# LayerNorm on GpSimd as scale and add in a fused attention and GLU block, with a re-planned instruction order

## The chip, the cores and the metric

The kernel runs on one core of one Trainium2 chip. The time is the device time of one execution in microseconds; the time before is the median of three runs, 234.61 us (234.28 to 237.68). One further execution was taken by the profiler; its span is 233.8 us and its own time 235.49 us.

## The reference, cut to what matters

One transformer block on x of 2048 rows and 512 columns in bf16: an adaptive LayerNorm (scale and shift come from a vector c through `w_mod`), linear attention with 32 heads of 16 whose feature map is a pair of softmaxes, a second adaptive LayerNorm, and a gated linear unit with 1376 hidden columns.

```python
h = layernorm(x) * (1 + ca) + sa              # (x - m) / sqrt(v + eps), then scale, shift
q, k, v = split(h @ wqkv)                     # 32 heads of 16
phi(t) = [softmax(t @ w_phi), softmax(-t @ w_phi)]
kv, z = phi(k)^T v, sum of phi(k) over rows
x = x + ga * ((phi(q) kv) / (phi(q) z + 1e-6)) @ wo
h = layernorm(x) * (1 + cb) + sb
x = x + gb * (sigmoid(h @ w_gate) * (h @ w_up)) @ w_down
```

## The kernel before

The rows are cut into 16 tiles of 128 rows (t = 0 to 15). Everything stays in SBUF. The work falls into two parts.

The K/V loop goes over the tiles in nine groups (LG: tiles 0 and 1 alone, then pairs). For each tile: VectorE takes mean and variance (`st1`, L782 and L783, into `mv1`); a group's `rs1` = 1/sqrt(v + eps) is made by Ln and Exp on ScalarE (L789, L790) or by add and power on GpSimd (L792, L793); `nmr` = -mean x rs1 is made by VectorE (L799); the normalised tile `xn` is made on ScalarE (L808, as rs1 x + nmr), VectorE (L810) or GpSimd (L812), the last two as (x - mean) rs1. `xn` is transposed, by TensorE into PSUM (`tp_h`, L826) or by a DMA on SyncE's queue (L818) for groups 2, 6 and 7, and scaled and shifted into `h1T` in four pieces (L833 on ScalarE, L835 on VectorE or, for DMA groups, GpSimd). TensorE then makes K (L853, with w_phi folded into the weights, `fold_ps`, L758) and V (L857); ScalarE takes exp of +K and -K (`e`, L869); VectorE sums each head's 16 columns (`ks`, L872); the reciprocal is made on VectorE (L885) or as Ln and Exp on ScalarE (L882, L883); GpSimd multiplies (`phi`, L875), in NPART pieces for a tile; TensorE accumulates `kvacc` (L343) with `vaug`, a copy of V (L893). The buffers of `e` and `phi` come from a class of six (r2k), so few tiles are in flight. Matmuls on a zeroed weight tile (`warm`, L710) keep TensorE running at the start. modc (L722) is scale and shift of both LayerNorms; `bd` (L693) is the block diagonal of w_phi.

The second part goes over the tiles again: q and its exponentials (`q_ps` L927, `eT` L932), numerator and denominators (`num` L463, `sm` L438, `u` L469), the sum of both halves `o` on GpSimd (L487), its transposition by DMA (L490), the output projection (`a_ps` L496), the second LayerNorm, and the GLU in six chunks (`g_ps` and `u_ps` L581, `tg` L585, product L590, `y_ps` L604). GpSimd also scales wo by ga (L911) and w_down by gb (L916). At the end of the program stands a branch for inputs of a large range, which isn't taken.

Order and placement: every piece of work is a task with the engines it may run on and an estimated time for each (`alts`), a due time and a release time. `Graph.order` runs a list scheduler over them when the program is built: at each moment it takes the ready task of the earliest due time whose engine and buffers are free. The tables at the top (T0, KP, LGD, KD, UD, MISC, WARM and others) are due and release times; XN1, HM1 and RK say which engines each tile's `xn`, `h1T` pieces and reciprocals may use; XN1_T, and numbers in the calls of `G.add`, are the estimated times. On the chip each engine then runs its own list in order and waits by semaphores; the estimates matter there only through the order.

Of the kernel before, what the change touches and what calls it, by code (L numbers as in the profile page):

```python
# [56 lines left out]
KD = [47.89, 15.44, 5.38, 21.3, -5.65, -2.7, -0.87]
LGD = [4.09, -2.99, 1.74, 8.75, 21.66, 5.51, 6.02, -0.76, -1.68]
GSL = [4.41, 1.07, 0.25, 0.64, 1.79, 10.29]
UD = [-1.67, 1.09, -8.4, -21.5, 10.53, -7.46, 32.4, -7.3, -2.67]  # L60
MISC = [25.74, 36.7, 47.58, 53.98, -8.92, 22.77, 51.62]
# [163 lines left out]
def kernel(  # L225
# [550 lines left out]
    for g, ts in enumerate(LG):  # L776
# [18 lines left out]
        nmr_used = any(e == "ACT" for t in ts for e in XN1[t])  # L795
        if nmr_used:
            def f_nm(e, ts=ts):
                for t in ts:
                    dve.tensor_scalar(nmr[:, 0, t:t + 1], mv1[:, t, 0:1], rs1[:, t:t + 1], -1.0, op0=ALU.mult, op1=ALU.mult)  # L799
            G.add(f"nmr1_{g}", {"DVE": 0.07 * n}, f_nm,  # L800
                  r=[("rs1", g)], w=[("nmr1", g)], due=gd)
        for t in ts:
            xn = Buf("xn", [P, D], BF16, "xn")
            xns.append(xn)

            def f_xn(e, t=t, xn=xn):
                if e == "ACT":
                    act.activation(xn[:], x_sb[:, t, :], ACT.Identity, scale=rs1[:, t:t + 1], bias=nmr[:, 0, t:t + 1])  # L808
                elif e == "DVE":
                    dve.tensor_scalar(xn[:], x_sb[:, t, :], mv1[:, t, 0:1], rs1[:, t:t + 1], op0=ALU.subtract, op1=ALU.mult)  # L810
                else:
                    pool.tensor_scalar(xn[:], x_sb[:, t, :], mv1[:, t, 0:1], rs1[:, t:t + 1], op0=ALU.subtract, op1=ALU.mult)  # L812
# [228 lines left out]
```

## Time and profile before

| what | value |
|---|---|
| median of three runs | 234.61 us (234.28 to 237.68) |
| the profiled execution: time, span | 235.49 us, 233.8 us |
| TensorE busy | 208.6 us, 89% of the span |
| VectorE busy | 163.9 us, 70% |
| ScalarE busy | 108.6 us, 46% |
| GpSimd busy | 107.9 us, 46% |
| DMA moved | 19.02 MB, mean 81 GB/s |

The page cuts the span into 40 slices and gives each engine's busy share in a slice in tenths. Busy shares over the whole span mix the two parts, so stages are read one by one. In rows of instructions the columns are line, engine, operation, output and inputs with their shapes, count, then busy time in us, mean ns of one, and the idle time of the engine just before them with what ended it. Rows of the timeline begin with start and duration in us. SPq is SyncE's DMA queue, PEld TensorE's weight loads.

### The profile page before, as it was taken

The numbers are of one execution on the slowest core, as the hardware profiler recorded it, in microseconds if no ns is written. First come the engines' busy times: TensorE is split into PE (matmuls) and PEld (weight loads), VectorE is DVE, ScalarE is ACT, GpSimd is POOL, SyncE is SP. The second block draws the span as 40 slices with busy tenths as digits, with TensorE's granted clock in tenths as the row PEclk, the third lists the DMA queues.
The fourth block names the chain that finished last, engine by engine and source line by source line (L and its number), as shares of the span: only waits on it lengthen the run. The fifth ranks groups of instructions, "written<-read, shape, count | busy, mean of one in ns | idle before, by whom it ended". The sixth has DMA issues, their size and how long they took to land.

```text
span 233.8 us, 4338 instructions
## 1 busy us (share of the span) xinstructions
PE 208.6 (89%) x1559; PEld 115.8 (50%) x1583; DVE 163.9 (70%) x380; ACT 108.6 (46%) x247; POOL 107.9 (46%) x115
## 2 busy tenths in 40 slices
PE   7694793897899997999999998999999999999990
PEld 2452441633454664786776453444465444444460
DVE  3199885954873799997887678858879886334330
ACT  4298882787695988453272321442232150343100
POOL 4759999999999829785110044200004510000000
PEclk9999999599999999999999999999999999999998
DMA  6974691059600002006222023031002224000011
...
DMA packets 31455, 19.02 MB, mean 81 GB/s; under 512 B 21729, under 2 KB 29378, under 8 KB 31426
## 3 DMA queue, kind: packets, MB, share of 16 engines
...
q8 instruction: 14, 0.23, 0.4%
...
q10 hardware_dynamic: 530, 0.02, 0.1%
...
## 4 chain that ended last, share of the span: by engine, by line
PE 51%; POOL 16%; issue 10%; DVE 10%; ACT 9%; DMA 2%; POOLq 0%; DVEq 0%; ACTq 0%; SPq 0%
PE y_ps L604 14%; PE g_ps L581 13%; PE u_ps L581 13%; POOL phi L875 7%; POOL xn L812 6%; PE a_ps L496 4%; ACT e L869 3%; PE warm L710 3%; DVE u L469 2%; DMA oT<-o 2%; ACT eT L932 2%; DVE st L505 1%; DVE x L501 1%; PE num L463 1%; PE k_ps L853 1%
## 5 line engine op out<-in xcount | busy, mean ns | idle before, releaser
L585 ACT ACTIVATE tg<-g_ps 128x512 bf16<-128x512 f32 (+5 forms) x66 | 29.4, 453 | 71.2 <-PE g_ps L581 59.9
L590 DVE SCALAR_TENSOR_TENSOR wmod_sb<-tg,u_ps 128x512 bf16<-128x512 bf16 (+5 forms) x66 | 31.8, 503 | 18.5 <-PE u_ps L581 16.9
L604 PE MATMUL y_ps<-wd_sb,wmod_sb 128*128 128x512 bf16 (+2 forms) x180 | 43.7, 366 | 0.3
L487 POOL TENSOR_TENSOR o<-u 128x512 bf16<-128x512 f32 x14 | 17.5, 1270 | 50.2 <-DVE u L469 50.2
L581 PEld LDWEIGHTS <-wg_sb 128*128 128x128 bf16 (+1 forms) x264 | 23.8, 100 | 18.4
L875 POOL TENSOR_TENSOR phi<-e,ks 128x1024 bf16<-128x1024 bf16 (+2 forms) x21 | 31.4, 1512 | 0.5
L581 PEld LDWEIGHTS <-wu_sb 128*128 128x128 bf16 (+1 forms) x264 | 23.5, 100 | 15.7
L581 PE MATMUL g_ps<-wT_sb,wg_sb 128*128 128x512 bf16 (+3 forms) x130 | 26.7, 325 | 0.2
L581 PE MATMUL u_ps<-wT_sb,wu_sb 128*128 128x512 bf16 (+3 forms) x130 | 26.6, 325 | 0.1
L872 DVE TENSOR_REDUCE ks<-e 128x64 f32<-128x1024 bf16 (+2 forms) x21 | 19.6, 952 | 9.8 <-POOL phi L875 5.2
L812 POOL TENSOR_SCALAR xn<-x_sb,mv,rs 128x512 bf16<-128x512 bf16 x12 | 24.9, 2076 | 3.1 <-ACT rs L790 2.7
L604 PEld LDWEIGHTS <-wmod_sb 128*128 128x128 bf16 (+1 forms) x187 | 17.8, 98 | 16.4
L869 ACT ACTIVATE e<-k_ps 128x512 bf16<-128x512 f32 (+2 forms) x42 | 17.7, 507 | 10.0 <-POOL phi L875 6.7
L581 PE MATMUL g_ps<-wqk_sb,wg_sb 128*128 128x128 bf16 (+5 forms) x132 | 22.1, 290 | 0.1
L581 PE MATMUL u_ps<-wqk_sb,wu_sb 128*128 128x128 bf16 (+5 forms) x131 | 21.9, 290 | 0.1
L469 DVE TENSOR_TENSOR u<-num,cc 128x512 f32<-128x512 f32 (+1 forms) x32 | 20.2, 682 | 0.8 <-PE num L463 0.6
L613 DVE TENSOR_TENSOR ot<-y_ps,x 128x512 bf16<-128x512 f32 (+1 forms) x17 | 11.2, 657 | 11.1 <-PE y_ps L604 11.1
L853 PE MATMUL k_ps<-wqk_f,h1T 128*128 128x512 bf16 x59 | 16.3, 391 | 0.8 <-DVE h1T L835 0.5
L932 ACT ACTIVATE eT<-q_ps 128x512 bf16<-128x512 f32 x32 | 16.5, 615 | 0.8 <-PE q_ps L927 0.8
L496 PE MATMUL a_ps<-wo_sb,oT 128*128 128x512 bf16 x62 | 16.0, 380 | 0.9 <-DMA oT<-o 0.6
L857 PE MATMUL v_ps<-wv_sb,h1T 128*128 128x512 bf16 x63 | 16.3, 384 | 0.1
L343 PE MATMUL kvacc<-vaug,phi 128*128 128x68 bf16 x128 | 7.8, 208 | 8.3 <-POOL phi L875 8.2
(128 smaller groups left out, 286.4 us busy)
## 6 DMA issues: line engine op xcount, KB each, us to landing
...
x_sb<-in_A_x_dram SPq DMA_DIRECT2D x3, 512.0 KB, 9.2
...
wqk_sb<-in_A_wqkv_dram SPq DMA_DIRECT2D x2, 512.0 KB, 7.2
wmod_sb<-in_w_mod_dram SPq DMA_DIRECT2D x2, 512.0 KB, 6.5
```

Source lines behind the costliest of these rows:

```text
L469: dve.tensor_tensor(u[:], ps[:].rearrange("p (h d) -> p h d", d=DH), cc[:, q, s, :].unsqueeze(2).to_broadcast([P, H, DH]), op=ALU.mult)
L496: pe.matmul(ap_[:], lhsT=oT[:, j, :], rhs=wo_sb[:, j, :], start=(j == 0), stop=(j == KT - 1))
L581: pe.matmul(ps[:fsz, 0:n], lhsT=w[:, j, ft * P:ft * P + fsz], rhs=h[:, j, 0:n], start=(j == 0), stop=(j == KT - 1))
L585: G.add(f"tg{k}.{ft}", {"ACT": 0.13 + n * 0.00083}, lambda e, tg=tg, g_ps=g_ps, fsz=fsz, n=n: act.activation(tg[:fsz, 0:n], g_ps[:fsz, 0:n ...
L590: dve.scalar_tensor_tensor(hm_all[:fsz, hm[k].slot, ft, 0:n], tg[:fsz, 0:n], 1.0, u_ps[:fsz, 0:n], op0=ALU.add, op1=ALU.mult)
L604: pe.matmul(y[:, 0:c1 - c0], lhsT=hm_all[:fsz, hm[k].slot, ft, tl * P:(tl + 1) * P], rhs=wd_sb[:fsz, ft, c0:c1], start=(ft == 0), stop=(ft ...
L812: pool.tensor_scalar(xn[:], x_sb[:, t, :], mv1[:, t, 0:1], rs1[:, t:t + 1], op0=ALU.subtract, op1=ALU.mult)
L853: pe.matmul(kp[:], lhsT=h1T[:, j, t * P:(t + 1) * P], rhs=wqk_f[:, j, D:2 * D], start=(j == 0), stop=(j == KT - 1))
L869: act.activation(ee[:, ha:hb, s, :], kp[:, ha * DH:hb * DH].rearrange("p (h j) -> p h j", j=DH), ACT.Exp, scale=1.0 - 2.0 * s)
L872: dve.tensor_reduce(ks[:, ha:hb].rearrange("p h s -> p (h s)"), ee[:, ha:hb].rearrange("p h s j -> p (h s) j"), axis=AX.X, op=ALU.add)
L875: pool.tensor_tensor(ph[:, ha * 32:hb * 32].rearrange("p (h j) -> p h j", j=DH), ee[:, ha:hb].rearrange("p h s j -> p (h s) j"), ks[:, ha: ...
L932: act.activation(eT[cq][:, s * 4 + blk, :], qp[:], ACT.Exp, scale=1.0 - 2.0 * s)
```

## The change

On GpSimd the first LayerNorm is now rs1 x + nmr, one instruction with multiply and add, as ScalarE already does it. So nmr is needed by every tile that may run on GpSimd, and such a task waits for it. Some estimated times are new (xn on each engine, nmr, the two GpSimd tasks `perm` and `wo`, the exponentials of q), and the tables of due times, releases and allowed engines have new values throughout. The changed file is two lines shorter, so its lines stand two earlier.

```diff
@@ -27,43 +27,41 @@
-NPART = [1, 1, 1, 1, 1, 1, 1, 1, 1, 1, 1, 1, 2, 1, 2, 4]
-T0, KP, GL = 10.3, 3.07, -8.17
-WARM = [1.2, 2.75, 5.27, 2.7, 1.2, 4.52, 5.28, 2.92, 1.75, 3.49, 8.85, 6.48, 10.34, 8.21, 7.83, 6.77]
+NPART = [1, 1, 1, 1, 1, 1, 1, 1, 1, 1, 1, 4, 1, 2, 2, 2]
+T0, KP, GL = 12.02, 3.1, -9.09
+WARM = [1.51, 4.09, 5.7, 3.33, 1.89, 2.68, 5.52, 2.14, 1.2, 5.18, 8.38, 9.39, 9.77, 13.05, 8.64, 8.5]
...
 XN1 = [
-    ['POOL', 'ACT'], ['POOL'], ['POOL', 'ACT'], ['DVE', 'POOL', 'ACT'], ['DVE', 'POOL', 'ACT'], ['DVE', 'POOL'], ['POOL', 'DVE'], ['DVE', 'ACT'],
-    ['POOL', 'DVE', 'ACT'], ['POOL'], ['ACT', 'DVE'], ['POOL'], ['POOL', 'ACT', 'DVE'], ['DVE', 'ACT', 'POOL'], ['DVE', 'POOL'],
-    ['ACT', 'POOL', 'DVE'],
+    ['DVE'], ['ACT', 'POOL', 'DVE'], ['ACT', 'DVE', 'POOL'], ['POOL'], ['POOL', 'DVE', 'ACT'], ['POOL', 'ACT', 'DVE'], ['DVE', 'POOL'],
+    ['POOL', 'ACT', 'DVE'], ['ACT', 'DVE', 'POOL'], ['POOL'], ['POOL'], ['POOL'], ['ACT', 'DVE', 'POOL'], ['POOL', 'ACT', 'DVE'],
+    ['POOL', 'DVE', 'ACT'], ['ACT'],
 ]
-XN1_T = {"ACT": 0.75, "POOL": 0.8, "DVE": 0.33}
+XN1_T = {"ACT": 0.73, "POOL": 0.69, "DVE": 0.3}
...
@@ -792,12 +790,12 @@
                 pool.tensor_scalar(ve1[:, sl], mv1[:, sl, 1], 1e-5, None, op0=ALU.add)
                 pool.tensor_tensor(rs1[:, sl], ve1[:, sl], mhalf[:, sl], op=ALU.pow)
         G.add(f"rs1_{g}", RS1[g], f_rs, r=[("mv1", t) for t in ts], w=[("rs1", g)], due=gd)
-        nmr_used = any(e == "ACT" for t in ts for e in XN1[t])
+        nmr_used = any(e != "DVE" for t in ts for e in XN1[t])
         if nmr_used:
             def f_nm(e, ts=ts):
                 for t in ts:
                     dve.tensor_scalar(nmr[:, 0, t:t + 1], mv1[:, t, 0:1], rs1[:, t:t + 1], -1.0, op0=ALU.mult, op1=ALU.mult)
-            G.add(f"nmr1_{g}", {"DVE": 0.07 * n}, f_nm,
+            G.add(f"nmr1_{g}", {"DVE": 0.02 + 0.1 * n}, f_nm,
                   r=[("rs1", g)], w=[("nmr1", g)], due=gd)
         for t in ts:
             xn = Buf("xn", [P, D], BF16, "xn")
@@ -809,9 +807,9 @@
                 elif e == "DVE":
                     dve.tensor_scalar(xn[:], x_sb[:, t, :], mv1[:, t, 0:1], rs1[:, t:t + 1], op0=ALU.subtract, op1=ALU.mult)
                 else:
-                    pool.tensor_scalar(xn[:], x_sb[:, t, :], mv1[:, t, 0:1], rs1[:, t:t + 1], op0=ALU.subtract, op1=ALU.mult)
+                    pool.tensor_scalar(xn[:], x_sb[:, t, :], rs1[:, t:t + 1], nmr[:, 0, t:t + 1], op0=ALU.mult, op1=ALU.add)
             alts = {e: XN1_T[e] for e in XN1[t]}
-            G.add(f"xn1_{t}", alts, f_xn, r=[("rs1", g)] + ([("nmr1", g)] if "ACT" in alts else []), w=[("xn1", t)],
+            G.add(f"xn1_{t}", alts, f_xn, r=[("rs1", g)] + ([("nmr1", g)] if set(alts) != {"DVE"} else []), w=[("xn1", t)],
                   bufs=[xn], due=gd, port=("POOL", "DVE"))
```

The rest of the diff holds new values of LGD, KD, UD, HM1, RK and the like, and three estimates: `perm` 0.7 to 1.3, `wo` 1.28 to 1.1, the exponentials of q 1.2 to 1.0.

What the scheduler makes of it is read from the instruction lists. Of the 16 xn GpSimd had 12 and ScalarE 4; now GpSimd has 9, ScalarE 5 and VectorE 2 (tiles 0 and 1). Both lists hold 15 nmr. GpSimd makes rs1 for four groups (before: three) and two h1T pieces (before: four). phi has 12 whole tiles, six halves and four quarters; before 13, four and four.

GpSimd's list at the start of the K/V loop, from the block diagonal bd on. Before:

```order
L693 TENSOR_TENSOR bd<-wp_sb,bmask 128x512
L812 TENSOR_SCALAR xn<-x_sb,mv_78,rs_80 128x512 x3
L792 TENSOR_SCALAR ve_79<-mv_78 128x2
L793 TENSOR_TENSOR rs_80<-ve_79,mhalf 128x2
L812 TENSOR_SCALAR xn<-x_sb,mv_78,rs_80 128x512
L875 TENSOR_TENSOR phi<-e,ks 128x1024
L835 TENSOR_SCALAR h1T<-h1T,modc 128x256
L875 TENSOR_TENSOR phi<-e,ks 128x1024
L812 TENSOR_SCALAR xn<-x_sb,mv_78,rs_80 128x512
L792 TENSOR_SCALAR ve_79<-mv_78 128x2
L793 TENSOR_TENSOR rs_80<-ve_79,mhalf 128x2
L812 TENSOR_SCALAR xn<-x_sb,mv_78,rs_80 128x512
```

Now:

```order
L691 TENSOR_TENSOR bd<-wp_sb,bmask 128x512
L810 TENSOR_SCALAR xn<-x_sb,rs_80,nmr 128x512 x2
L790 TENSOR_SCALAR ve_79<-mv_78 128x2
L791 TENSOR_TENSOR rs_80<-ve_79,mhalf 128x2
L790 TENSOR_SCALAR ve_79<-mv_78 128x2
L791 TENSOR_TENSOR rs_80<-ve_79,mhalf 128x2
L810 TENSOR_SCALAR xn<-x_sb,rs_80,nmr 128x512
L873 TENSOR_TENSOR phi<-e,ks 128x1024 x2
L810 TENSOR_SCALAR xn<-x_sb,rs_80,nmr 128x512 x5
L790 TENSOR_SCALAR ve_79<-mv_78 128x2
L791 TENSOR_TENSOR rs_80<-ve_79,mhalf 128x2
L873 TENSOR_TENSOR phi<-e,ks 128x1024 x4
```

Two xn, not three, stand first (those of tiles 0 and 1 have gone to VectorE), and a third waits behind two rs; behind the first two phi five xn stand in a row, and then four phi, where xn and phi took turns before.

VectorE's list at the same place, from the statistics of an early tile to the second sum for phi (ks). Before:

```order
L782 BN_STATS st_77<-x_sb 128x6
L783 BN_AGGR mv_78<-st_77 128x2
L799 TENSOR_SCALAR nmr<-mv_78,rs_80 128x1 x2
L782 BN_STATS st_77<-x_sb 128x6
L783 BN_AGGR mv_78<-st_77 128x2
L872 TENSOR_REDUCE ks<-e 128x64
L893 CAST vaug_104<-v_ps 128x32x16
L799 TENSOR_SCALAR nmr<-mv_78,rs_80 128x1 x2
L782 BN_STATS st_77<-x_sb 128x6
L783 BN_AGGR mv_78<-st_77 128x2
L872 TENSOR_REDUCE ks<-e 128x64
```

Now:

```order
L797 TENSOR_SCALAR nmr<-mv_78,rs_80 128x1 x2
L780 BN_STATS st_77<-x_sb 128x6
L781 BN_AGGR mv_78<-st_77 128x2
L780 BN_STATS st_77<-x_sb 128x6
L781 BN_AGGR mv_78<-st_77 128x2
L780 BN_STATS st_77<-x_sb 128x6
L781 BN_AGGR mv_78<-st_77 128x2
L870 TENSOR_REDUCE ks<-e 128x64
L797 TENSOR_SCALAR nmr<-mv_78,rs_80 128x1 x2
L870 TENSOR_REDUCE ks<-e 128x64
L797 TENSOR_SCALAR nmr<-mv_78,rs_80 128x1 x2
L883 RECIPROCAL ks<-ks 128x64
```

The nmr of the two pairs whose rs1 GpSimd makes now stand behind one ks each. Ahead of this piece VectorE makes the xn of tiles 0 and 1, the second behind its two copies of wT_sb.

TensorE's list at the same place goes over tile pairs: V0, V1, K0, K1, then (after warm matmuls and transposes) kvacc of tile 0, V2, V3, kvacc of tile 1, the transposes of tiles 6 and 7, K2, K3. Before it was K0, V0, K1, V1, and later kvacc of tile 0, K2, kvacc of tile 1, V2.

GpSimd's list behind the loop, from the scalings of wo on, now:

```order
L909 TENSOR_TENSOR wo_sb<-wo_sb,ga_sb 128x512 x4
L914 TENSOR_TENSOR wd_sb<-wd_sb,wmod_sb 128x512 x7
L485 TENSOR_TENSOR o<-u 128x512 x2
L514 TENSOR_SCALAR ve_83<-mv_82 128x1
L515 TENSOR_TENSOR rs_84<-ve_83,mhalf 128x1
L914 TENSOR_TENSOR wd_sb<-wd_sb,wmod_sb 128x512 x4
```

Seven scalings of wd_sb (L914) stand ahead of the first two o, where there were two; behind them rs of tile 1 for the second LayerNorm and the other four scalings.

More of the change, by code (lines that the diff above doesn't have):

```diff
@@ L52 @@
 ]
 RK = [
-    ['ACT'], ['DVE', 'ACT'], ['ACT'], ['DVE'], ['ACT'], ['DVE', 'ACT'], ['ACT'], ['DVE'], ['ACT'], ['DVE'], ['DVE'], ['DVE', 'ACT'], ['DVE'],
-    ['ACT'], ['ACT', 'DVE'], ['DVE'],
-]
[L57 to L61, printed above, removed]
+    ['ACT'], ['ACT', 'DVE'], ['DVE'], ['ACT'], ['ACT', 'DVE'], ['DVE', 'ACT'], ['ACT'], ['DVE'], ['ACT', 'DVE'], ['ACT', 'DVE'], ['ACT'],
@@ L62 @@
+    ['DVE', 'ACT'], ['ACT', 'DVE'], ['ACT', 'DVE'], ['DVE', 'ACT'], ['ACT', 'DVE'],
+]
+KD = [48.44, 11.65, 6.7, 25.12, -3.51, -11.2, -0.78]
+LGD = [2.92, -6.82, 9.16, -1.34, 23.14, 16.31, 0.7, 11.25, -7.18]
+GSL = [2.48, 1.14, 0.29, 0.81, 0.08, 3.45]
+UD = [-1.67, 5.7, 7.31, -25.78, 8.16, -6.86, 23.5, -7.3, 15.4]
+MISC = [25.41, 35.64, 49.36, 52.17, -11.34, 27.03, 44.33]
 TD = [0, 0, 1, 0, 0, 0, 1, 1, 0]
@@ L65 @@
 ENG = {}
-WDREL, WDDUE, WDSTEP = 71.41, 142.51, 0.01
+WDREL, WDDUE, WDSTEP = 65.72, 186.99, -0.81
 class Buf:
@@ L356, in f @@
                     pool.tensor_copy(bd[:, 2 * s + h, h * 64:(h + 1) * 64].rearrange("p (h j) -> p h j", j=DH), iv[:, :, s, :])
-        G.add("perm", {"POOL": 0.7}, f, w=["bd"], due=due, rel=rel)
+        G.add("perm", {"POOL": 1.3}, f, w=["bd"], due=due, rel=rel)
     def kvbd_tasks(G, acc):
@@ L910 @@
     for j in range(KT):
-        G.add(f"wo{j}", {"POOL": 1.28}, lambda e, j=j: engine(e).tensor_tensor(wo_sb[:, j, :], wo_sb[:, j, :], ga_sb[:], op=ALU.mult),
+        G.add(f"wo{j}", {"POOL": 1.1}, lambda e, j=j: engine(e).tensor_tensor(wo_sb[:, j, :], wo_sb[:, j, :], ga_sb[:], op=ALU.mult),
               r=["gac", "wo_raw"], w=[("wo", j)], bufs=[ga_sb], due=GB + MISC[5], rel=50.0)
@@ L934 @@
             G.add(f"Q{cq}{blk}", {"PE": 0.87}, f_q, r=[("h1", g, j) for g in range(len(LG)) if LG[g][0] // 4 == cq for j in range(KT)] + [("wqk", j, 0) for j in range(KT)], w=[("q", cq, blk)], bufs=[qp], due=due, rel=QREL[cq])
-            G.add(f"qe{cq}{blk}", {"ACT": 1.2}, f_qe, r=[("q", cq, blk)], w=[("eT", cq, blk)], bufs=[qp, eT[cq]], due=due)
+            G.add(f"qe{cq}{blk}", {"ACT": 1.0}, f_qe, r=[("q", cq, blk)], w=[("eT", cq, blk)], bufs=[qp, eT[cq]], due=due)
     downstream(G, eT, GB, True)
```

18 lines of the change are left out of this document (8 added, 10 removed).

## The prediction

> **What bounds the kernel now.** I read the slices and the chain of the page first, then busy time by stage, then the waits of the first 90 us.
>
> ```profile
> POOL 4759999999999829785110044200004510000000
> PE 51%; POOL 16%; issue 10%; DVE 10%; ACT 9%; DMA 2%; POOLq 0%; DVEq 0%; ACTq 0%; SPq 0%
> ```
> ```profile
> core 0: us, PE busy (x) PEld busy (x) DVE busy (x) ACT busy (x) POOL busy (x), PEclk, DMA share, GB/s
> 15.40:73.10 57.70, 45.15 (x354) 23.59 (x358) 42.18 (x92) 42.33 (x104) 56.67 (x41) 0.94 0.48 145
> 73.60:97.30 23.70, 21.67 (x243) 14.26 (x245) 21.04 (x51) 18.91 (x42) 17.95 (x21) 1.00 0.06 12
> 97.30:228.60 131.30, 129.55 (x868) 71.60 (x879) 93.58 (x218) 39.63 (x81) 24.80 (x29) 1.00 0.19 42
> 40.00:50.00 10.00, 7.77 (x91) 5.07 (x93) 7.68 (x16) 7.93 (x22) 9.92 (x7) 0.66 0.14 29
> ```
> ```profile
> PE kvacc L343 <- POOL phi L875: 8.2, 8, 4.0
> ACT e L869 <- POOL phi L875: 6.7, 2, 4.2
> DVE ks L872 <- POOL phi L875: 5.2, 4, 3.2
> ```
>
> The kernel has two parts. From 73.6 on, TensorE sets the end: 21.67 of 23.70 us busy, then 129.55 of 131.30. In the K/V loop, 15.40 to 73.10, GpSimd does: 56.67 of 57.70 us, while the other three are busy for 42 to 45 us and wait for phi, the GpSimd product. TensorE's work is the same either way, so what shortens the loop should move everything behind it forward.
>
> **What GpSimd does in the loop.** Groups by form: count, busy us, mean ns, idle before.
>
> ```profile
> L875 POOL TENSOR_TENSOR phi<-e,ks 128x1024 bf16<-128x1024 bf16 x13 | 25.0, 1927 | 0.3
> L875 POOL TENSOR_TENSOR phi<-e,ks 128x512 bf16<-128x512 bf16 x4 | 4.1, 1055 | 0.2
> L875 POOL TENSOR_TENSOR phi<-e,ks 128x256 bf16<-128x256 bf16 x4 | 2.4, 618 | 0.0
> L812 POOL TENSOR_SCALAR xn<-x_sb,mv,rs 128x512 bf16<-128x512 bf16 x12 | 24.9, 2076 | 3.1 <-ACT rs L790 2.7
> L835 POOL TENSOR_SCALAR h1T<-h1T,modc 128x256 bf16<-128x256 bf16 x4 | 2.2, 555 | 0.0
> L793 POOL TENSOR_TENSOR rs<-ve,mhalf 128x2 f32<-128x2 f32 x3 | 2.2, 718 | 0.3
> L516 POOL TENSOR_SCALAR ve<-mv 128x2 f32<-128x2 f32 x7 | 1.5, 220 | 23.8 <-DVE mv L506 23.8
> ```
>
> Ten of the twelve xn fall behind 15.40: 10 x 2.076 = 20.8; phi 25.0 + 4.1 + 2.4 = 31.5; h1T 2.2; three times rs with its add of eps, 3 x 0.94 = 2.8. Sum 57.3, the whole window. So a microsecond off GpSimd here is a microsecond off the loop, until another engine is as long.
>
> **The price of the new xn.** No row shows scale-and-add at 128x512. The nearest is h1T on the same engine: the same instruction with two per-partition fp32 operands, bf16 in and out, multiply then add, at 256 columns 555 ns; subtract then multiply costs 2076 at 512. Twice the columns cannot make 3.7 times the time, so the pair of operations must carry most of it. Below: the line through the 2-column add (220 ns) and h1T gives 555 + 256 x 335/254 = 893 ns. Above: twice h1T, 1110, and if the shape rather than the operations is slow, 2076. I take 950, nearest to the line. As a side note, the Trainium skill (GPSIMD Engine Reference, section 3.1, Elementwise) gives one-input loops a best case of 769 ns for 512 elements, whatever the operation; by that the nine xn would cost 6.9 us, not 8.6. The 2076 row shows that operation pairs do differ here, which the page does not say.
>
> **What moves.** On GpSimd 12 xn become 9 (3 x 2.076 and 9 x 1.126 saved), h1T pieces 4 become 2, rs groups 3 become 4; phi has 12 whole, 6 half and 4 quarter tiles, 31.9 us. From 57.3 + 2 x 2.076 = 61.5 us the queue shrinks to 8.6 + 31.9 + 1.1 + 3.8 = 45.4.
>
> The offsets cost nothing new: 15 of them stand in the trace and 15 in the changed order.
>
> ```profile
> L799 DVE TENSOR_SCALAR nmr<-mv,rs 128x1 f32<-128x1 f32 x15 | 2.4, 198 | 0.7 <-POOL rs L793 0.7
> L872 DVE TENSOR_REDUCE ks<-e 128x64 f32<-128x1024 bf16 x13 | 15.6, 1203 | 9.1 <-ACT e L869 4.6 <-POOL phi L875 4.5
> L808 ACT ACTIVATE xn<-x_sb,nmr,rs 128x512 bf16<-128x512 bf16 x4 | 3.2, 806 | 0.0
> L893 DVE CAST vaug<-v_ps 128x512 bf16<-128x512 f32 x7 | 4.8, 682 | 1.7 <-PE v_ps L857 1.4 <-PE kvacc L343 0.2
> L882 ACT ACTIVATE ks<-ks 128x64 f32<-128x64 f32 x7 | 1.9, 269 | 0.0
> ```
>
> What is new is the wait: xn on GpSimd now needs VectorE after rs, and nmr stands behind a ks reduction (1.2 us) in VectorE's queue. Behind the waiting xn stand the next phi, and for those TensorE's kvacc.
>
> VectorE gets two xn, one vaug cast (L893) and three more h1T pieces from SBUF; ScalarE one xn (0.81) and three reciprocals by Ln and Exp (two instructions of 0.27). Each adds 2 to 3 us to 42 us of work in a 57.7 us loop: hidden, and on the path once the loop nears 45 us.
>
> ```profile
> 52.64 4.13 POOL L812 TENSOR_SCALAR xn<-x_sb,mv,rs 128x512 bf16<-128x512 bf16 x2
> 53.42 0.34 DVE L835 TENSOR_SCALAR h1T<-h1T,modc 128x256 bf16<-128x256 bf16 x1
> ```
>
> A h1T piece took 0.34 us on VectorE in the middle of two GpSimd xn, so I charge two xn at most 0.68 each and three pieces 0.34. The Trainium skill (SBUF — State Buffer, section Who interferes with whom) says that a VectorE tensor_scalar in a two-port mode and a GpSimd instruction exclude each other for a whole instruction; by that each of the five could wait up to one phi, 9.6 us of VectorE in all. These two rows show no such wait.
>
> **Head.** Before, TensorE stood in order behind the first xn:
>
> ```profile
> 1.82 1.01 SPq L661 DMA_DIRECT2D wmod_sb<-in_w_mod_dram  x2
> 7.36 1.15 POOL L693 TENSOR_TENSOR bd<-wp_sb,bmask 128x512 bf16<-128x512 bf16 x1 [3.70 <-DMA wp_sb<-in_A_w_phi_dram]
> 7.56 0.87 DVE L747 COPY wT_sb<-tp_w 128x512 bf16<-128x512 bf16 x2 [1.56 <-PE tp_w L741]
> 10.65 0.29 PE L826 MATMUL tp_h<-ident,xn 128*128 128x128 bf16 x2 [2.02 <-POOL xn L812]
> 11.28 0.83 PE L758 MATMUL fold_ps<-bd,wT_sb 128*128 128x128 bf16 x12
> 13.26 1.54 ACT L833 ACTIVATE h1T<-tp_h,modc 128x128 bf16<-128x128 bf16 x4
> 14.62 1.03 PE L853 MATMUL k_ps<-wqk_f,h1T 128*128 128x512 bf16 x3
> 15.40 2.07 POOL L812 TENSOR_SCALAR xn<-x_sb,mv,rs 128x512 bf16<-128x512 bf16 x1 [2.74 <-ACT rs L790]
> ```
> ```profile
> wmod_sb<-in_w_mod_dram SPq DMA_DIRECT2D x2, 512.0 KB, 6.5
> ```
>
> With both first xn on VectorE, the second after its wT_sb copies at 8.4, what is left is wmod_sb (landed 6.5 after its issue, by 9.3) and bd (8.5): the folds start at about 9.5 instead of 11.28 and the first projection at 13. But V0 and V1 now stand ahead of K0 and K1, so K0 ends near 15.5, its exponentials at 16.8, its reduction at 18.3. GpSimd: two xn from 14.8 to 16.7, two rs to 18.6, a third xn (behind nmr, behind that reduction) to 19.7, phi0 to 21.6, phi1 to 23.5. Estimates, all from the rows above.
>
> **Sum.** After phi1 GpSimd has six xn (5.7), two rs (1.9), ten whole phi (19.3), six halves (6.3), four quarters (2.5), two h1T (1.1): 36.8 us. TensorE, from K2 at 25.0 (behind kvacc 1 and the transposes of the first of five xn in a row):
>
> ```profile
> 64.61 3.62 PE L927 MATMUL q_ps<-h1T,wqk_f 128*128 128x512 bf16 x16
> 68.06 0.67 PE L343 MATMUL kvacc<-vaug,phi 128*128 128x68 bf16 x16
> 68.57 1.02 PE L857 MATMUL v_ps<-wv_sb,h1T 128*128 128x512 bf16 x4
> 60.63 12.55 POOL L875 TENSOR_TENSOR phi<-e,ks 128x1024 bf16<-128x1024 bf16 x11
> 73.59 0.23 PE L343 MATMUL kvacc<-vaug,phi 128*128 128x68 bf16 x2
> 41.20 0.64 PE L343 MATMUL kvacc<-vaug,phi 128*128 128x68 bf16 x8 [4.04 <-POOL phi L875]
> ```
>
> By starts, a 512-wide matmul is 3.45/16 = 0.216 us and a kvacc 0.51/16 = 0.032: 128 x 0.216 + 112 x 0.032 + some 3.4 for transposes, folds and modc = 34.6, to 59.6 if it never waits. GpSimd would end at 60.3. With the two so close, neither can be full: I give GpSimd a share of 0.90, as TensorE has (0.914) where TensorE, VectorE and ScalarE are all loaded, in the row from 73.60. 23.5 + 36.8/0.90 + 0.4 (last phi to last kvacc, as 73.18 to 73.59 now) = 64.8 against 73.6: 8.8 us earlier. Share 0.98 (GpSimd's now) gives 61.5, share 0.82 gives 68.8. At 1.11 us an xn it is 1.1 later.
>
> Behind the loop I charge nothing: the same matmuls follow, but for four of q (0.86 us) that stood ahead of the last kvacc and now fill the wait behind it. GpSimd runs seven wd_sb scalings ahead of the first o where there were two; five more are 6.0 us, against the 5.1 it waited there for u, so under 1 us, with TensorE's q matmuls as cover. Weight loads come forward with the loop.
>
> Span 233.8 - 8.8 = 225.0; the profiled execution took 235.49, 1.69 more than its span and 0.88 more than the median of 234.61. So **225.8 us**, its own range 222.5 to 229.8.
>
> **Rivals.** *The offset's detour (0.17).* POOL, DVE, POOL: of the five offset pairs behind phi1 each stands behind a reduction and keeps GpSimd 1.2 us: 6.0, loop end 70.8, 231.8 us. For it: nmr waited for rs already (0.7). Against: five xn stand in a row, so one wait can serve several.
>
> *The price stays (0.08).* If the shape is slow, phi1 ends at 26.9 and 43.6 us follow at share 0.98: end 71.8, 232.8 us. Against: the h1T row.
>
> *Better (0.07).* GpSimd stays as full as now, or xn costs under 0.89: 222.5 and less.
>
> *Slower: TensorE's clock (0.06).* Before 41.20 TensorE idled 4.04 us, and the row from 40 to 50 shows 0.66 of its clock. That was free while GpSimd was the bound; it is not once TensorE's 34.6 us are as long. At 0.60 through the loop they take 57.7: end 82.7 + 0.4, 244 us. It decides below 34.6/48.6 = 0.71. Against: the whole loop had 0.94. The Trainium skill (TensorE: Matmul & The Clock Gate, Part 1) puts the drop to half after about 3.4 us of idling; the 4.04 us row and the 0.66 agree; by that rule each such wait costs some 3 us more of TensorE.
>
> **The numbers.** Forecast 0.62, the rivals as given. Range 222 to 232: from the full share to the detour; outside are most of "price stays", the clock and a little of "better". A change of 2% (4.7 us) is about what a measurement can tell here. Faster by over 2%: forecast, "better" and 0.05 of milder detours, 0.74; within 2%: 0.20; slower: 0.06.
>
> **What would show it.** Right: xn on GpSimd near 0.95 us nine times; GpSimd's share of the loop near 0.9; the last kvacc near 65; 73.60:97.30 and 97.30:228.60 of unchanged length, moved forward. Wrong: xn at 2 us; GpSimd idle for nmr; TensorE idle 4 us before a kvacc and a clock under 0.8 there; or a loop that ends near 65 and a TensorE that then waits for u or o, giving it back.

## The result, and the profile after

| | before | after |
|---|---|---|
| median | 234.50 us (4 runs, 234.28 to 237.68) | 224.80 us (4 runs, 224.43 to 225.91) |
| profiled execution, its span | 235.49, 233.8 us | 224.43, 222.7 us |
| last kvacc starts | 73.59 | 61.81 |
| first g_ps starts | 94.70 | 83.48 |

After over before on one chip is 0.956, 95% interval 0.948 to 0.965: faster. The forecast was 225.8 us. In the runs below, a median counts every execution, and a ratio leaves out those in a slower state (227.36 us in the run on the head, 229.28 us in the run with the roots on ScalarE, and some of the kernel before). Lines behind about L700 are two lower than before (xn on GpSimd was L812, is L810).

The page after: GpSimd's busy tenths in 40 slices, and the chain that ended last, by engine.

```profile
POOL 4259799599999994321104032102214100000000
PE 61%; DVE 13%; POOL 10%; issue 5%; DMA 5%; ACT 3%; ACTq 0%; SPq 0%; POOLq 0%; DVEq 0%
```

Before, GpSimd stood at nine tenths or more without a break from slice 4 to 13. Now a slice is 5.6 us, the loop ends in slice 12, and there are a 7 and a 5 within it; the nines behind it are mostly scalings of weights. The chain has gone over to TensorE: 61% for 51%, GpSimd 10% for 16%. Busy time by stage:

```profile
core 0: us, PE busy (x) PEld busy (x) DVE busy (x) ACT busy (x) POOL busy (x), PEclk, DMA share, GB/s
11.90:23.90 12.00, 9.17 (x59) 4.45 (x57) 11.49 (x33) 9.70 (x22) 9.79 (x12) 0.86 0.77 181
23.90:61.90 38.00, 35.45 (x310) 18.86 (x308) 33.62 (x65) 33.62 (x91) 33.32 (x31) 1.00 0.62 196
```

In the row from 23.90 no engine is full and none is far from it: 35.45, 33.62, 33.62 and 33.32 of 38.00 us. Before, GpSimd alone was at 0.98 and the others at 0.73 to 0.78. TensorE's clock is 1.00 there. But these are means over 38 us, and shorter stretches of the same execution look different:

```profile
9.30:34.00 24.70, 21.01 (x148) 10.80 (x145) 24.00 (x60) 22.16 (x53) 17.78 (x19) 0.93 0.92 247
42.75:61.70 18.95, 18.05 (x174) 9.54 (x172) 15.83 (x32) 15.65 (x51) 18.71 (x17) 1.00 0.29 98
```

Up to 34.00 VectorE is full, 24.00 of 24.70 us; from 42.75 on GpSimd is, 18.71 of 18.95, with TensorE close behind.

GpSimd's groups by form, in the loop:

```profile
L810 POOL TENSOR_SCALAR xn<-x_sb,rs,nmr 128x512 bf16<-128x512 bf16 x9 | 6.9, 773 | 6.8 <-DVE nmr L797 6.7
L873 POOL TENSOR_TENSOR phi<-e,ks 128x1024 bf16<-128x1024 bf16 x12 | 22.9, 1931 | 2.9 <-DVE ks L883 2.2 <-ACT ks L881 0.6
L873 POOL TENSOR_TENSOR phi<-e,ks 128x512 bf16<-128x512 bf16 x6 | 6.2, 1059 | 0.2
```

The normalisation takes 773 ns where it took 2076, and phi costs what it did. The idle column is the new wait for nmr, 6.7 us; lines picked from the timeline say where it lies (start, duration, count, and in brackets the idle time before and its releaser).

```profile
8.66 0.83 PE L756 MATMUL fold_ps<-bd,wT_sb 128*128 128x128 bf16 x12 [0.37 <-POOL bd L691]
11.99 1.89 PE L855 MATMUL v_ps<-wv_sb,h1T 128*128 128x512 bf16 x8
13.62 1.53 POOL L810 TENSOR_SCALAR xn<-x_sb,rs,nmr 128x512 bf16<-128x512 bf16 x2 [5.01 <-DVE nmr L797]
18.11 3.81 POOL L873 TENSOR_TENSOR phi<-e,ks 128x1024 bf16<-128x1024 bf16 x2
21.91 2.40 POOL L810 TENSOR_SCALAR xn<-x_sb,rs,nmr 128x512 bf16<-128x512 bf16 x3
25.78 1.52 POOL L810 TENSOR_SCALAR xn<-x_sb,rs,nmr 128x512 bf16<-128x512 bf16 x2 [1.47 <-DVE nmr L797]
42.75 1.93 POOL L873 TENSOR_TENSOR phi<-e,ks 128x1024 bf16<-128x1024 bf16 x1 [2.18 <-DVE ks L883]
45.39 16.36 POOL L873 TENSOR_TENSOR phi<-e,ks 128x1024 bf16<-128x1024 bf16 x14
61.81 0.30 PE L341 MATMUL kvacc<-vaug,phi 128*128 128x68 bf16 x4
67.48 7.91 POOL L914 TENSOR_TENSOR wd_sb<-wd_sb,wmod_sb 128x512 bf16<-128x512 bf16 x7
75.33 2.53 POOL L485 TENSOR_TENSOR o<-u 128x512 bf16<-128x512 f32 x2
```

5.0 of the 6.7 us are the time before GpSimd's first xn, when it had nothing else; behind phi1 (the second phi) the wait for nmr is 1.47 us, once, in the stretch where VectorE is full. From 45.39 on GpSimd runs fourteen phi without a gap. Behind the last kvacc almost nothing changed: 94.70 - 73.59 = 21.1 us to the first g_ps before, 83.48 - 61.81 = 21.7 now, then 139.1 and 139.2 us to the end of the span. GpSimd runs its seven wd_sb scalings there and goes on to the first o with no wait for u. So the loop ends 11.8 us earlier, 0.6 is given back behind it, and the span is 11.1 shorter.

One more view, the durations of h1T between 36 and 40 us (min/median/max), and GpSimd beside it:

```profile
L833 DVE TENSOR_SCALAR h1T<-h1T,modc x4: 335/398/1982, 36.8 to 37.7; 128x256 bf16<-128x256 bf16 x4
37.66 1.92 POOL L873 TENSOR_TENSOR phi<-e,ks 128x1024 bf16<-128x1024 bf16 x1
```

Three of VectorE's four pieces take some 0.4 us. The fourth starts at 37.7, as phi does, and takes 1.98 us, as long as phi. In the head, VectorE's second xn (128x512) did likewise: 1.22 us from 7.54, while GpSimd's bd product ran from 7.46 to 8.61; the first had taken 0.38.

### The profile page after: what moved, and what is told of

The parts are those of the page before. It is cut to its first block, busy times and chain, and to the rows that moved or that the text cites. A ratio compares the mean times of both kernels' runs of the same rounds, so it can differ in the third digit from the quotient of the medians.

```text
span 222.7 us, 4366 instructions
## 1 busy us (share of the span) xinstructions
PE 207.2 (93%) x1583; PEld 115.3 (52%) x1583; DVE 166.7 (75%) x384; ACT 109.0 (49%) x253; POOL 90.1 (40%) x113
## 3 DMA queue, kind: packets, MB, share of 16 engines
q1 hardware_dynamic: 30896, 18.65, 31.5%
## 4 chain that ended last, share of the span: by engine, by line
PE 61%; DVE 13%; POOL 10%; issue 5%; DMA 5%; ACT 3%; ACTq 0%; SPq 0%; POOLq 0%; DVEq 0%
PE y_ps L602 16%; PE g_ps L579 15%; PE u_ps L579 15%; POOL phi L873 8%; PE a_ps L494 5%; DMA wp_sb<-in_A_w_phi_dram 3%; PE v_ps L855 3%; DVE ks L870 2%; DVE u L467 2%; DMA oT<-o 2%; PE num L461 2%; DVE st L780 2%; ACT e L867 1%; DVE st L503 1%; PE q_ps L925 1%
## 5 line engine op out<-in xcount | busy, mean ns | idle before, releaser
L588 DVE SCALAR_TENSOR_TENSOR wmod_sb<-tg,u_ps 128x512 bf16<-128x512 bf16 (+5 forms) x66 | 32.3, 504 | 21.2 <-PE u_ps L579 19.7
L602 PE MATMUL y_ps<-wd_sb,wmod_sb 128*128 128x512 bf16 (+3 forms) x187 | 45.6, 366 | 0.0
L579 PEld LDWEIGHTS <-wu_sb 128*128 128x128 bf16 (+1 forms) x264 | 23.5, 100 | 15.8
L851 PE MATMUL k_ps<-wqk_f,h1T 128*128 128x512 bf16 x64 | 15.1, 379 | 0.3 <-ACT h1T L831 0.3
L925 PE MATMUL q_ps<-h1T,wqk_f 128*128 128x512 bf16 x64 | 15.3, 379 | 0.0
L914 POOL TENSOR_TENSOR wd_sb<-wd_sb,wmod_sb 128x512 bf16<-128x512 bf16 x11 | 12.8, 1208 | 0.0
```

The source lines that it names most:

```text
L579: pe.matmul(ps[:fsz, 0:n], lhsT=w[:, j, ft * P:ft * P + fsz], rhs=h[:, j, 0:n], start=(j == 0), stop=(j == KT - 1))
L588: dve.scalar_tensor_tensor(hm_all[:fsz, hm[k].slot, ft, 0:n], tg[:fsz, 0:n], 1.0, u_ps[:fsz, 0:n], op0=ALU.add, op1=ALU.mult)
L602: pe.matmul(y[:, 0:c1 - c0], lhsT=hm_all[:fsz, hm[k].slot, ft, tl * P:(tl + 1) * P], rhs=wd_sb[:fsz, ft, c0:c1], start=(ft == 0), stop=(ft ...
L925: pe.matmul(qp[:], lhsT=wqk_f[:, j, blk * P:(blk + 1) * P], rhs=h1T[:, j, cq * 512:(cq + 1) * 512], start=(j == 0), stop=(j == KT - 1))
```

## The experiments

Two theories stood against each other first: the price of the operation pair made the gain, or the new order did (it moves three xn off GpSimd and re-plans the rest).

**The new order with the old operation.**

```diff
-pool.tensor_scalar(xn[:], x_sb[:, t, :], rs1[:, t:t + 1], nmr[:, 0, t:t + 1], op0=ALU.mult, op1=ALU.add)
+pool.tensor_scalar(xn[:], x_sb[:, t, :], mv1[:, t, 0:1], rs1[:, t:t + 1], op0=ALU.subtract, op1=ALU.mult)
```

> The changed kernel with its instruction order kept on every engine, and only GpSimd's nine xn set back to subtract and multiply (so they no longer wait for nmr). Theory (the price of the operation pair carries the gain): the nine cost 2.08 instead of 0.77 us, 11.7 us more on GpSimd; its 43.4 us of work in the loop become 55.1, full at a share of 0.98 from 13.6 on, loop end near 70 instead of 61.7, time 233 us (231 to 235). Rival (the new order and placement carry it): 225 to 227 us.

Measured: 233.93 us, 0.994 of before (0.990 to 0.998). Its GpSimd group and its last kvacc:

```profile
L810 POOL TENSOR_SCALAR xn<-x_sb,mv,rs 128x512 bf16<-128x512 bf16 x9 | 18.6, 2081 | 5.9 <-ACT rs L788 5.9
```
```profile
70.79 0.30 PE L341 MATMUL kvacc<-vaug,phi 128*128 128x68 bf16 x4
```

The new order alone is worth about 1 us. Between this kernel and the changed one GpSimd's queue is the same but for the price, 9 x (2.08 - 0.77) = 11.8 us; the loop ends 9.0 us later. So a microsecond of GpSimd was worth 0.76 there.

**The old order with the new operation.** The operation is exchanged in the kernel before, and the offset of a group is issued ahead of the first GpSimd xn that needs it (so xn is L820 and kvacc L349 here).

```diff
-pool.tensor_scalar(xn[:], x_sb[:, t, :], mv1[:, t, 0:1], rs1[:, t:t + 1], op0=ALU.subtract, op1=ALU.mult)
+pool.tensor_scalar(xn[:], x_sb[:, t, :], rs1[:, t:t + 1], nmr[:, 0, t:t + 1], op0=ALU.mult, op1=ALU.add)
```

> The kernel before with its order kept on every engine, and only GpSimd's twelve xn set to multiply and add; the nmr of a group stands ahead of its first such xn where it stood later, and tile 1 gets one. Theory (price): GpSimd's 57.3 us in the loop lose 10 x 1.30 = 13.0; at a share of 0.90 the loop takes 49 instead of 57.7 us, time 226 us (225 to 229, the upper end because the order was laid out for other waits). Rival (order): 232 to 235 us.

Measured: 226.13 us, 0.956 (0.947 to 0.964).

```profile
L820 POOL TENSOR_SCALAR xn<-x_sb,rs,nmr 128x512 bf16<-128x512 bf16 x12 | 9.2, 767 | 9.2 <-DVE nmr L805 8.1 <-issue 1.2
```
```profile
63.88 0.23 PE L349 MATMUL kvacc<-vaug,phi 128*128 128x68 bf16 x2
```

The operation alone brings 8.9 of some 10 us, in the order of before. The rival, the order, falls on both runs.

**Prices by themselves.** A small kernel in place of the block: four GpSimd tensor_scalars in a row for each pair of operations, and VectorE's scale-and-add alone and beside GpSimd.

```python
for n in (512, 256):
    for o0, o1 in ((S, M), (M, A), (M, S), (S, A), (A, M), (M, M)):
...
            for _ in range(4):
                pool.tensor_scalar(ya[:, 0:n], x_sb[:, 0, 0:n], s[0], s[1], op0=o0, op1=o1)
```

> Prices alone: GpSimd tensor_scalar on bf16 with two per-partition operands in six pairs of operations at 512 columns and two at 256, four in a row each; then a VectorE scale-and-add of 256 and of 512 columns in SBUF alone and beside GpSimd's subtract-multiply, multiply-add and phi. The block's computation is left out. Theory (operation pair): subtract-multiply 2.07 at 512, multiply-add 0.77, at 256 about 1.1 and 0.55. Rival (shape): both pairs alike at 512. Port: if a fast GpSimd instruction shuts VectorE out for its whole length, VectorE's rows grow to 0.7 and more beside multiply-add and phi, while beside subtract-multiply they stay near 0.34; if there is no such exclusion, all stay at their time alone.

Its timeline: subtract-multiply, multiply-add and multiply-multiply at 512 columns, then subtract-multiply and multiply-add at 256.

```profile
4.41 8.62 POOL L54 TENSOR_SCALAR ya<-x_sb,tok 128x512 bf16<-128x512 bf16 x4 [3.16 <-DVE tok L50]
13.46 3.39 POOL L54 TENSOR_SCALAR ya<-x_sb,tok 128x512 bf16<-128x512 bf16 x4 [0.44 <-DVE tok L50]
...
39.19 3.39 POOL L54 TENSOR_SCALAR ya<-x_sb,tok 128x512 bf16<-128x512 bf16 x4 [0.43 <-DVE tok L50]
43.02 5.19 POOL L54 TENSOR_SCALAR ya<-x_sb,tok 128x256 bf16<-128x256 bf16 x4 [0.43 <-DVE tok L50]
48.64 2.53 POOL L54 TENSOR_SCALAR ya<-x_sb,tok 128x256 bf16<-128x256 bf16 x4 [0.44 <-DVE tok L50]
```

8.62/4 = 2.16 us against 0.85 at 512, 1.30 against 0.63 at 256 (here each writes what the one before wrote; whether that is why these stand above the 0.77 of the kernel was not tried). Multiply-subtract and subtract-add took 8.61 us as well, add-multiply 3.38: each pair that holds a subtraction is slow, wherever it stands, and the shape is not the cause.

VectorE's 256-column pieces: six alone, eight beside GpSimd's subtract-multiply, eight beside its multiply-add, eight beside phi; that phi; and the durations of single pieces (min/median/max) beside multiply-add and beside phi.

```profile
51.48 2.26 DVE L70 TENSOR_SCALAR za<-x_sb,tok 128x256 bf16<-128x256 bf16 x6
54.04 3.69 DVE L70 TENSOR_SCALAR za<-x_sb,tok 128x256 bf16<-128x256 bf16 x8
63.22 3.88 DVE L70 TENSOR_SCALAR za<-x_sb,tok 128x256 bf16<-128x256 bf16 x8
67.47 9.48 DVE L70 TENSOR_SCALAR za<-x_sb,tok 128x256 bf16<-128x256 bf16 x8
67.78 7.94 POOL L66 TENSOR_TENSOR yb<-big,ks 128x1024 bf16<-128x1024 bf16 x4
L70 DVE TENSOR_SCALAR za<-x_sb,tok x8: 346/433/683, 63.2 to 66.6; 128x256 bf16<-128x256 bf16 x8
L70 DVE TENSOR_SCALAR za<-x_sb,tok x8: 346/1140/1970, 67.5 to 76.6; 128x256 bf16<-128x256 bf16 x8
```

By these stretches a piece costs 0.38 us alone, and 0.46 and 0.49 beside the two tensor_scalars, where single pieces took up to 0.68. Beside phi the mean of 1.19 stands for two kinds: four pieces took 1.93 to 1.97 us each, as long as a phi, and the other four, one ahead of the phi and three behind, 0.35. Phi itself does not suffer: 1.93 us each, as in the block.

**The head.** The changed order put the first two xn on VectorE.

```diff
-    ['DVE'], ['ACT', 'POOL', 'DVE'], ...
+    ['POOL'], ['POOL'], ...
```

GpSimd's queue differs by these two alone; VectorE loses them, and on TensorE the transposes of tile 0 and 1 change places with modc and warm-up matmuls.

> The changed kernel with the xn of tiles 0 and 1 on GpSimd instead of VectorE and the rest of the order as it was. Theory (the head counts): the transposes of tile 0 then wait for bd and one xn on GpSimd, to 9.4 instead of 7.1, and TensorE's folds behind them move from 8.66 to about 10.2; the whole loop starts 1.4 us later, 226.2 us (225.6 to 227). Rival (the head is hidden by GpSimd's and VectorE's work in the loop): 224.5 to 225.2 us.

Measured: 224.08 us, 0.949 (0.939 to 0.959).

```profile
61.67 0.30 PE L341 MATMUL kvacc<-vaug,phi 128*128 128x68 bf16 x4
```

The time is not longer and the loop ends no later. But the head did not move as the theory had it:

```profile
8.79 0.83 PE L756 MATMUL fold_ps<-bd,wT_sb 128*128 128x128 bf16 x12
```

The folds start at 8.79 us, against 8.66 in the changed kernel and 10.2 expected, and the first projection at 12.12, against 11.99. In this execution wp_sb landed 4.2 us after its issue, in the changed kernel's 6.0; so GpSimd made bd from 5.62 instead of 7.46, and had room for the two xn. So two xn more on GpSimd cost nothing here; whether a head that starts later would count was not put to the test.

**What holds the loop now.** With GpSimd no longer full, TensorE at 35.45 of 38.00 us looked like the new bound. Four kernels add or take work on one engine, in the changed order.

```diff
-                    pool.tensor_scalar(xn[:], ..., op0=ALU.mult, op1=ALU.add)
+                    [pool.tensor_scalar(xn[:], ..., op0=ALU.mult, op1=ALU.add) for _ in range(2)]
```

> The changed kernel, with each of the nine GpSimd normalisations issued twice in a row (the second writes the same values again): 9 x 0.77 = 6.9 us more for GpSimd, everything else in the same order. In the changed kernel TensorE is busy for 35.45 of the 38.0 us from 23.9 to 61.9, GpSimd for 33.3. Theory 'TensorE is the bound there, GpSimd has room of some 4 us': last kvacc 2.5 to 4 us later, near 65, 227 to 228.5 us. Rival, the prediction's own picture 'GpSimd is the bound, at a share of 0.90 that stays': last kvacc 6.9 to 7.7 later, near 69, 231 to 232.5 us.

```diff
-            for j in range(KT):
-                pe.matmul(kp[:], ..., start=(j == 0), stop=(j == KT - 1))
+            for i, j in enumerate([0, *range(KT)]):
+                pe.matmul(kp[:], ..., start=(j == 0), stop=(i in (0, KT)))
```

> The changed kernel, with one 512-wide matmul more ahead of each of the 16 K projections (its result is overwritten): 16 x 0.216 = 3.5 us more for TensorE in the loop, the same order elsewhere. Theory 'TensorE is the bound': last kvacc 3 to 3.5 us later, near 65, 227.3 to 228.3 us. Rival 'GpSimd is the bound': under 1 us later, 224.5 to 225.5 us.

```diff
         def f_rs(e, sl=sl):
-            if e == "ACT":
+            if True:
                 act.activation(ve1[:, sl], mv1[:, sl, 1], ACT.Ln, bias=eps[:, 0:1])
```

> The changed kernel, with the four reciprocal roots of the block that GpSimd computes moved to ScalarE at the same places of the program: GpSimd loses 4 x 0.94 = 3.8 us (two before phi1, two behind), ScalarE gains 8 instructions of 0.2 to 0.3, some 2 us. Theory 'TensorE is the bound': last kvacc less than 1.2 us earlier, 223.2 to 225 us. Rival 'GpSimd is the bound': last kvacc 3 to 4 us earlier, 220.4 to 221.5 us.

```diff
-            for j in range(KT):
-                pe.matmul(vp[:], ..., start=(j == 0), stop=(j == KT - 1))
+            for j in range(KT - 1):
+                pe.matmul(vp[:], ..., start=(j == 0), stop=(j == KT - 2))
```

> The changed kernel, whose V projections leave out their last of four matmuls (a quarter of the sum for V is not computed): 16 x 0.216 = 3.5 us less for TensorE in the loop, the same order. Theory 'TensorE is the bound': last kvacc 1.5 to 3.5 us earlier (GpSimd's 35.7 us of work stand behind it as the next bound), 221 to 223 us. Rival 'GpSimd is the bound': under 0.7 us earlier, 223.8 to 224.8 us.

| kernel | GpSimd | TensorE | last kvacc | median us | ratio to before (95%) |
|---|---|---|---|---|---|
| changed | | | 61.81 | 224.80 | 0.956 (0.948 to 0.965) |
| xn twice | +6.9 | | 67.35 | 229.86 | 0.981 (0.974 to 0.988) |
| a matmul more | | +3.5 | 63.08 | 225.37 | 0.960 (0.955 to 0.966) |
| roots on ScalarE | -3.8 | | 62.89 | 225.52 | 0.959 (0.953 to 0.966) |
| a matmul less | | -3.5 | 62.67 | 225.37 | 0.960 (0.954 to 0.966) |

The last kvacc of the four, in the order of the table:

```profile
67.35 0.30 PE L341 MATMUL kvacc<-vaug,phi 128*128 128x68 bf16 x4
```
```profile
63.08 0.30 PE L341 MATMUL kvacc<-vaug,phi 128*128 128x68 bf16 x4
```
```profile
62.89 0.30 PE L341 MATMUL kvacc<-vaug,phi 128*128 128x68 bf16 x4
```
```profile
62.67 0.30 PE L341 MATMUL kvacc<-vaug,phi 128*128 128x68 bf16 x4
```

Neither theory holds as it was put. More GpSimd work costs 5.5/6.9 = 0.80 of itself, between the two expectations; less gains nothing (though here ScalarE took on some 2 us). More TensorE work ends the loop 1.3 us later where "TensorE is the bound" wanted 3 to 3.5, and the kernels with less work on GpSimd or on TensorE end it 1.1 and 0.9 us later as well. The kernel with a matmul less doesn't settle what TensorE weighs, because its clock fell. The same 16 K matmuls, in the changed kernel and in this one:

```profile
47.65 3.61 PE L851 MATMUL k_ps<-wqk_f,h1T 128*128 128x512 bf16 x16
```
```profile
47.33 5.30 PE L851 MATMUL k_ps<-wqk_f,h1T 128*128 128x512 bf16 x16
```

They took 1.7 us longer; the granted clock from 44 to 54 was 0.83, in the changed kernel 1.00. That is half of the 3.5 us that were taken off. The ratios of the three kernels near 225.4 cannot be told from the changed kernel's, and of their 0.9 to 1.3 us in the last kvacc a good part may be chance: the first phi's start alone lies between 17.97 and 18.65 in runs whose head is the same.

**VectorE behind phi.** Does the piece that phi shut out for 2 us set anything? VectorE's five SBUF pieces of h1T go to ScalarE, or to GpSimd.

```diff
-                if e == "ACT":
+                if e == "ACT" or (tp is None and e == "DVE"):
```

> The changed kernel, with VectorE's five SBUF pieces of h1T given to ScalarE at the same places of the program. In the changed kernel four of them start at 36.81 and end at 39.67, 0.1 us after the phi that GpSimd ran from 37.66 to 39.58, and 2.2 us of GpSimd's waiting follow (phi at 42.75). Theory 'VectorE shut out by phi costs the loop some 1.1 us there': VectorE is free for its vaug casts 2 us sooner, but ScalarE has 5 x 0.6 = 3.0 us more: last kvacc from 1 us earlier to 1 us later, 223.5 to 225.5 us. Rival 'a chain through all four engines that any added work lengthens': last kvacc 1 to 2.5 us later, 225.5 to 227 us.

```diff
-                    engine(e).tensor_scalar(dst, src, ..., op0=ALU.mult, op1=ALU.add)
+                    (pool if tp is None else dve).tensor_scalar(dst, src, ..., op0=ALU.mult, op1=ALU.add)
```

> The changed kernel, with VectorE's five SBUF pieces of h1T given to GpSimd at the same places: 5 x 0.58 = 2.9 us more for GpSimd, no VectorE piece left that phi can shut out. Theory 'VectorE shut out by phi costs the loop some 1.1 us there': the 2.2 us for which GpSimd waited at 42.75 take up four of the pieces, and VectorE's reductions come up to 1.1 us sooner: last kvacc 0 to 1.1 us earlier, 223.3 to 224.5 us. Rival 'a chain through all four engines that any added work lengthens': last kvacc 0.7 to 2 us later, 225.2 to 226.5 us.

Measured: 225.80 us, 0.958 (0.952 to 0.965), and 225.29 us, 0.955 (0.949 to 0.962). The first's last kvacc starts at 62.95; the second's, and its busy time from 24 to 29 us:

```profile
63.62 0.30 PE L341 MATMUL kvacc<-vaug,phi 128*128 128x68 bf16 x4
```
```profile
24.00:29.00 5.00, 4.84 (x31) 2.87 (x31) 3.29 (x10) 3.44 (x8) 3.31 (x6) 0.76 0.98 337
```

The first lies 1.1 us later, where the stall theory allowed 1 and the chain theory wanted 1 to 2.5, and says little. The second lies 1.8 later, inside the chain theory's 0.7 to 2, where the stall theory wanted 0 to 1.1 earlier. But TensorE's clock was 0.76 in this row, 1.00 in the changed kernel from 24 to 29, so part of the 1.8 may be the clock's; and its median is no different from the changed kernel's. No gain shows from freeing VectorE of the stall, at the price of the same work elsewhere. What the stall alone costs stays open.

**Relief without a burden.** The last pair takes work off and adds none. (In the expectations e12 is the first kernel of this pair, e9 the one with a matmul less.)

```diff
-              lhsT=ph[:, g * P:(g + 1) * P],
+              lhsT=ph[:, (g if len(parts) > 1 else g % 4) * P:][:, 0:P],
...
             def f_p(e, ee=ee, ks=ks, ph=ph, ha=ha, hb=hb):
+                hb = hb if hb - ha < 32 else 16
```

> The changed kernel, in which GpSimd computes only the first half of phi for the twelve whole tiles and TensorE reads that half twice (the other half of these products is left out): 12 x (1.93 - 1.06) = 10.4 us less for GpSimd, spread over the whole loop, nothing added to another engine. Theory 'two engines equally long' (TensorE 35.5 and GpSimd 33.3 of 38.0 us): TensorE alone holds the loop, last kvacc 1 to 2.5 us earlier, 222.3 to 223.8 us. Rival 'GpSimd is the bound at a share of 0.90': last kvacc 8 to 11 us earlier, 214 to 217 us. Rival 'a chain of waits through all four engines in which each phi counts': 4 to 7 us earlier, 218 to 221 us.

> The kernel of e12 (half of phi left out for twelve tiles) whose V projections also leave out their last of four matmuls (as in e9): GpSimd 10.4 us shorter and TensorE 3.5 us. Theory 'two engines equally long': now both are relieved, last kvacc 2 to 3.5 us earlier than in e12, 219 to 221 us. Rival 'ScalarE and VectorE (33.6 of 38.0 us each) are as long, so a chain through all four': last kvacc within 1 us of that of e12.

Measured: 222.89 us, 0.948 (0.942 to 0.955), and 223.00 us, 0.947 (0.940 to 0.954). The first kernel's last kvacc and its loop:

```profile
59.97 0.30 PE L341 MATMUL kvacc<-vaug,phi 128*128 128x68 bf16 x4
```
```profile
23.90:59.00 35.10, 33.51 (x298) 18.55 (x301) 31.58 (x64) 32.94 (x90) 23.81 (x30) 1.00 0.71 212
```

The second's, at a clock of 0.98:

```profile
59.82 0.30 PE L341 MATMUL kvacc<-vaug,phi 128*128 128x68 bf16 x4
```
```profile
23.90:59.00 35.10, 31.77 (x286) 17.80 (x289) 31.77 (x64) 32.30 (x89) 23.95 (x30) 0.98 0.67 212
```

10.4 us off GpSimd bring the loop's end forward by 1.8 (one profiled execution each): some 0.18 of each microsecond. That refutes "GpSimd is the bound" for the loop of the changed kernel as a whole. With TensorE relieved as well, the end does not move (59.97, 59.82), so the theory of two engines equally long falls too. The last rival named ScalarE and VectorE; their means, 32.3 and 31.8 of 35.1 us, don't say where they count. Shorter stretches of the first kernel do:

```profile
9.30:34.00 24.70, 20.81 (x150) 10.87 (x149) 23.56 (x60) 21.79 (x52) 14.06 (x19) 0.93 0.92 248
29.00:49.00 20.00, 18.52 (x182) 10.80 (x184) 18.72 (x34) 19.69 (x51) 12.68 (x15) 1.00 1.00 287
```
```profile
51.23 8.69 POOL L873 TENSOR_TENSOR phi<-e,ks 128x256 bf16<-128x256 bf16 x10 [1.64 <-PE kvacc L341]
```

VectorE's last statistics, in the changed kernel and in this one:

```profile
33.32 0.68 DVE L780 BATCH_NORM_STATS2 st<-x_sb 128x6 f32<-128x512 bf16 x1
```
```profile
33.37 0.68 DVE L780 BATCH_NORM_STATS2 st<-x_sb 128x6 f32<-128x512 bf16 x1
```

Up to 34 us VectorE runs its list almost without a gap in both (24.00 and 23.56 of 24.70 us) and comes to its last statistics at the same moment; 3.7 us less GpSimd work in that stretch (17.78, 14.06) can't bring them forward. In the half-phi kernel ScalarE is full next, 19.69 of 20.00 us from 29 to 49. And at the end GpSimd is full again: from 51.23 it runs ten phi pieces (the six halves and four quarters) without a gap to 59.92, and the last kvacc starts at 59.97. The edit left these ten as they were; the twelve tiles that it relieved all lie ahead of them. So the relief was not spread over the whole loop, and GpSimd still sets the last 8.7 us. No engine holds the whole loop; each stretch has its own. That is read from the traces: no run shortened VectorE's work up to 34 or ScalarE's behind it by itself.

## Why the prediction was right, point by point

*GpSimd bounds the loop, TensorE the rest: right for the kernel before.* The stretch behind the loop kept its length within 0.6 us. "A microsecond off GpSimd is a microsecond off the loop" was too much: 0.76 to 0.80 in both kernels that have more GpSimd work than the changed one. In the changed kernel GpSimd sets the end of the loop only, from 42.75 on.

*The price, 0.95 us: too high.* It is 0.773, below the lower bound of 0.893. The line through a 2-column add and a 256-column h1T failed: h1T's 555 ns at 256 and xn's 773 at 512 give 0.85 ns a column, where that line had 1.32. Nine times 0.18 is 1.6 us, 1.1 of it behind phi1. The Trainium skill (GPSIMD Engine Reference, section 3.1, Elementwise) gives a best case of 769 ns for 512 elements and names no operation; the trace agrees with it for multiply-add (773 ns here, 767 in the old order), stands at 0.85 us for add-multiply and multiply-multiply with chained writes, and does not agree for pairs with a subtraction.

*The detour of nmr: rightly unlikely.* 1.5 us behind phi1, not 6.0.

*VectorE's additions: the working failed.* "Two xn at most 0.68 each and three pieces 0.34" was read from a piece beside two GpSimd xn. Beside GpSimd tensor_scalars that is near what the small kernel shows (0.46 and 0.49, single pieces up to 0.68). Beside a two-input product it is not: one xn took 1.22 us and one piece 1.98. The Trainium skill (SBUF — State Buffer, section Who interferes with whom) has a VectorE tensor_scalar in a two-port mode and a GpSimd instruction exclude each other for a whole instruction; these two rows agree, and so do the four pieces beside phi in the small kernel; the rows beside tensor_scalars do not. It happened twice, not five times, and cost some 2.4 us of VectorE, not 9.6. That VectorE's work is hidden, as the prediction had it until the loop nears 45 us, is not borne out up to 34.00, where VectorE is the full engine.

*The head: mis-sized.* Folds at 8.66, not 9.5, the first projection at 11.99, not 13, phi1's end at 21.9, not 23.5. Of the loop's end these are 1.6 us in the sum below; no run here delayed the head alone, so what it weighs by itself stays open.

*The sum: right number, wrong reason in part.* GpSimd's work behind phi1 is six xn 4.6, two rs 1.9, phi 19.3 + 6.4 + 2.5, h1T 1.2: 35.8 us, done from 21.9 to 61.7, a share of 0.90, as put. That it came to 0.90 is in part luck. The figure was borrowed from TensorE, in a stretch behind the loop, and GpSimd's own share was not even: 16.30 of 20.85 us from 21.90 to 42.75, where it waited for others, and 18.71 of 18.95 from there on. Nor is it a property of GpSimd: with 10.4 us less it falls to 23.81/35.10 = 0.68, because the loop hardly gets shorter. The new price had brought GpSimd's mean just to the level of the other three. The last kvacc at 61.81 instead of 64.8 is 1.6 for phi1's end, 1.1 for the shorter queue behind it (39.8 us, not 40.9) and 0.3 for the step from the last phi to the last kvacc (0.1, not 0.4); 0.6 went behind the loop, where nothing had been charged and up to 1 allowed. 225.0 - 3.0 + 0.6 = 222.6, and 222.7 was measured.

*The clock: rightly unlikely.* TensorE never waited over 1.1 us for phi behind phi0, and its clock was 1.00 from 23.90 to the loop's end and 0.86 in the stretch ahead of it; before, the loop had 0.94. The risk is real all the same: with a matmul less a stretch at 0.83 appeared and cost TensorE 1.7 us.
